# Retention attention and two MLP layers on one core: the last third of the first layer moved to a seven-product scheme, attention order, one slot pool

## The chip, the cores and the metric

One core of a Trainium2 chip runs the whole program in one launch. The metric is the device time of one execution in microseconds (us), lower is better. Engines: PE (TensorE, matmuls; PEld is its weight loads), DVE (VectorE), ACT (ScalarE), POOL (GpSimd), and SP, whose queue issues the DMAs. A line number such as L143 is a line of the kernel before; in the kernel after, the same statements stand some lines higher or lower.

## The reference

```python
# q, k, v: (4, 8, 576, 64)
gamma = 1.0 - 2.0 ** (-5.0 - np.arange(H))
Dmat = np.where(rel >= 0, gamma[:, None, None] ** rel, 0.0)   # rel = query - key position
x = ((q @ k^T) / 8 * Dmat) @ v                                # per batch and head, no softmax
x = x.transpose(0, 2, 1, 3).reshape(2304, 512)
h = x @ w_in ;  x = np.maximum(0.01 * h, h) @ w_out           # layer 1: 512 -> 2048 -> 512
h = x @ w2_in;  x = (h * sigmoid(h)) @ w2_out                 # layer 2, the same sizes
```

The weights arrive as float64 and are turned into float32 on the chip. All large matmuls are done at float32 precision by splitting each operand into a rounded part (hi) and a rest (lo) and adding three products, hi x hi, hi x lo, lo x hi (`PASSES`).

## The kernel before, in words

**Attention** works on eight units: for each of four batches the first 256 tokens (A) and the last 320 (B). A0 and A1 are done ahead of everything; the other six are cut into pieces (load, scale_k, products, outer, values) and put into the MLP's steps at the times in `ATT_AT` (L41). Its result goes into `X`, the 2304 tokens in the order of `UNITS` (L39), channels on partitions.

**Layer 1** runs over blocks of tokens, `BLOCKS` (L48): 512, 320, 512, 512, 448. A step is one block and one of the 16 slices f of the hidden layer: `gemm1` (L422, 12 matmuls into `h`), `activate` (L434: ACT leaky ReLU, ACT cast to hi, DVE rest lo into `g`), and `gemm2` two steps later (L444, 12 matmuls into `acc`). Each step also splits its two weight tiles, `wi` and `wo` (ACT cast, DVE subtraction; `split`, L119). In the first block the weights are also loaded and decoded (`decode`, L369). The first 32 steps stand in program order; from there to the end of the layer the scheduler chooses the order.

**Layer 2** takes 768 tokens at a time, three pairs of 384 (`PAIRS`, L30), in eight rounds k of two slices f each. The first product (X times w2_in) is done as a 2x2 block product with seven block products in place of eight: `sums_x` (L472) forms the sums of the X blocks and splits them, `sums_w` (L528) the same for the weights, `quad` (L576) issues the seven products of 6 matmuls x 384 columns into two PSUM banks `a` and `b`. Between products ACT copies bank `a` out (`snapshot`, L578), DVE adds bank `b` to such a copy (`add`, L584), and `finish` (L560) applies the activation and splits it into `gh` and `gl`. Snapshot, add and finish are marked high priority. A product that adds to bank `a` waits until the snapshot has read it. `outputs` (L614), 36 matmuls of 512 columns of the round before, fills the time between the products. PE and SP keep the program's order here; ACT and DVE are ordered by the scheduler. In the first pair the split weights are also written to DRAM (`kept`), and the later pairs fetch them from there. The weights of layer 2 are decoded in the last steps of layer 1 and in the first pair.

**Memory**: separate pools for raw weights, x splits, wi, wo, g, and after layer 1 new pools for the pairs (L847 to L851).

Of the kernel before, what the change touches and what calls it, by code (L numbers as in the profile page):

```python
# [22 lines left out]
LAG = 2  # L23
# [6 lines left out]
PAIRS = B * S // (2 * TILE)  # L30
# [17 lines left out]
BLOCKS = [[(0, 512), (512, 320), (832, 512), (1344, 512), (1856, 448)]]  # L48
# [15 lines left out]
def retention_mlp_kernel(ctx: ExitStack, tc: tile.TileContext, qkva, qkvb, w1, w2, consts, out):  # L64
# [4 lines left out]
    early = ctx.enter_context(ExitStack())  # L69
# [7 lines left out]
    wraw_p = pool("wraw", 1)  # L77
    x_p = pool("x", 1)
    xs_p = pool("xs", 6, stack=early)
    wi_p = pool("wi", 2, stack=early)  # L80
    wo_p = pool("wo", 2, stack=early)
    hs_p = pool("hs", 2, stack=early)
    g_p = pool("g", 3, stack=early)
    dec_p = pool("dec", 3, side=right)
    ld_p = pool("ld", 3, stack=heads, side=right)
# [6 lines left out]
    def slot(shape, dt, name, kind="wraw"):  # L92
        return wraw_p.tile(shape, dt, tag=kind, name=name, bufs={"wraw": NF - 7, "first": 7}[kind])
# [18 lines left out]
    gq2 = g_p.tile([128, NP, 2, CH], F32, tag="g", name="gq2")  # L112
# [73 lines left out]
    def products(u, ps):  # L186
# [29 lines left out]
        for i, p in enumerate(ps):  # L216
            k = [kv[p][:, c % 2, c // 2 * 64:(c // 2 + 1) * 64] for c in range(4)]
            if u[0] == "A":
                x = st_p.tile([128, 4, 64], F32, tag="st", name="st")
                sa = st_p.tile([128, 64], F32, tag="sa", name="sa", bufs=2 * NP)  # L220
# [58 lines left out]
    def end2(b, p, x):  # L279

        sa = st_p.tile([128, 64], F32, tag="sa", name="sa", bufs=2 * NP)
# [70 lines left out]
    def load_w(layer, f, parts=(0, 1)):  # L352

        if (layer, f) not in w64:
            wraw[layer, f] = slot([128, 1024], F32, "wraw", "first" if layer == 0 and f < 7 else "wraw")
# [44 lines left out]
    def split_wi(layer, i, f):  # L400

        w = wi_p.tile([128, 2, 512], F32R, tag="wi", name="wi")
# [3 lines left out]
    def split_wo(layer, i, f):  # L406

        w = wo_p.tile([128, 2, 512], F32R, tag="wo", name="wo")
# [3 lines left out]
    def split_x(layer, i, c, half=None, engine=nc.vector):  # L412
        p0, n = BLOCKS[layer][i]
        if not half:
            xs[layer, i, c] = xs_p.tile([128, 2, 512], F32R, tag="xs", name="xs")
# [6 lines left out]
    def gemm1(layer, i, f):  # L422
        n = BLOCKS[layer][i][1]
# [10 lines left out]
    def activate(layer, i, f):  # L434

        n = BLOCKS[layer][i][1]
        h = hidden.pop((layer, i, f))
        hs = hs_p.tile([128, 512], F32, tag="hs", name="hs")
        g = g_p.tile([128, 2, 512], F32R, tag="g", name="g")
# [4 lines left out]
    def gemm2(layer, i, f):  # L444
        p0, n = BLOCKS[layer][i]
# [26 lines left out]
    def sums_x(p):  # L472

        v = [[X[:, 2 * j:2 * j + 2, (2 * p + k) * TILE:(2 * p + k + 1) * TILE] for k in range(2)] for j in range(2)]
        b11, b12, b21, b22 = v[0][0], v[0][1], v[1][0], v[1][1]
        t1, t2, t4 = (xt_p.tile([128, 2, TILE], F32, tag="xt", name="xt") for _ in range(3))
        yield nc.vector.tensor_tensor(out=t1, in0=b12, in1=b11, op=ALU.subtract)
        yield nc.vector.tensor_tensor(out=b12, in0=b22, in1=b12, op=ALU.subtract)
        yield nc.vector.tensor_tensor(out=t2, in0=b22, in1=t1, op=ALU.subtract)
        yield nc.vector.tensor_tensor(out=t4, in0=b21, in1=t2, op=ALU.subtract)  # L480
        for name, x in (("b11", b11), ("b21", b21), ("t2", t2), ("t1", t1), ("t3", b12), ("t4", t4), ("b22", b22)):
            hi = xh_p.tile([128, 2, TILE], F32R, tag="xh", name="xh")
            yield nc.scalar.copy(out=hi, in_=x)
            lo = slot([128, 2, TILE], F32R, "xl", "first")
            yield nc.vector.tensor_tensor(out=lo, in0=x, in1=hi.bitcast(F32), op=ALU.subtract)
            xw[p, name] = hi, lo

    xw = {}
    ww = {}

# [4 lines left out]
    def weights(p, k):  # L495

        if (p, k) == (0, 0):
            homes = {"ha": (xt_p, "xt"), "la": (dec_p, "w64"), "hs": (xs_p, "xs"), "ls": (xs_p, "xs")}
        else:
            homes = {n: (wc_p, n) for n, _, _ in PARTS}  # L500
        t = {n: homes[n][0].tile([128, m, 256], F32R, tag=homes[n][1], name=n) for n, _, m in PARTS}
# [7 lines left out]
    def weights_out(p, k):  # L509

        wo = [wo2_p.tile([128, 2, 512], F32R, tag="wo", name="wo") for _ in range(2)]
        for i in range(2):
            wsp[1, p, 2 * k + i, 1] = wo[i]
            there = kept[k][:, 14 + 4 * i:18 + 4 * i]
            here = wo[i].bitcast(F32).rearrange("p a (b n) -> p (a b) n", b=2)
            if p:
                nc.sync.dma_start(out=here, in_=there)
            else:
                yield from split(wo[i][:, 0], wo[i][:, 1], wraw[1, 2 * k + i][:, 512:], nc.vector)
                nc.sync.dma_start(out=there, in_=here)  # L520
# [7 lines left out]
    def sums_w(p, k):  # L528
# [3 lines left out]
        w, z = wraw[1, 2 * k], wraw[1, 2 * k + 1]  # L532
        a = w[:, :512].rearrange("p (c n) -> p c n", c=2)
        yield nc.scalar.copy(out=ha[:, :2], in_=a)
        yield nc.vector.tensor_tensor(out=la[:, :2], in0=a, in1=ha[:, :2].bitcast(F32), op=ALU.subtract)
        s = [xt_p.tile([128, 2, 256], F32, tag="xt", name="ws") for _ in range(2)]
# [3 lines left out]
        yield nc.scalar.copy(out=hs[:, :2], in_=s[0])  # L540
# [406 lines left out]
```

## Time and profile before

| | us |
|---|---|
| median of 3 runs (lowest, highest) | 856.27 (856.17, 857.05) |
| the profiled execution: its own time | 856.27 |
| its span, first to last instruction | 854.4 |
| PE busy, of the span | 837.3 (98%) |
| DVE busy | 479.2 (56%) |
| ACT busy | 423.1 (50%) |
| POOL busy | 16.8 (2%) |

The profiled execution took 856.27 us, which is the median itself; 1.9 us of that lie outside the span. Busy shares are means over stages that differ: attention and decoding load DVE and ACT in the first 110 us and around the change from layer 1 to layer 2 (at about 464 us), and hardly in between or at the end.

### The profile page before, as it was taken

What the parts mean: (1) busy time and instruction counts of PE and PEld (TensorE: products, weight loads), DVE (VectorE), ACT (ScalarE), POOL (GpSimd) and SP (SyncE); (2) the same over time, 40 slices, a digit from 0 to 9 for tenths busy, and PEclk for the clock granted to TensorE, in tenths of its full rate; (3) what the DMA queues carried; (4) which work ended last, traced back from release to release, by engine and by line L of the source; (5) the groups of instructions that cost most, each with busy time, mean ns of one, the idle gap of its engine ahead of it and who ended that gap; (6) DMA issues with size and microseconds to landing.
All of it is one profiled execution on the core that took longest, in us unless ns stands there. A gap on an engine that the chain in (4) does not pass through costs nothing.

```text
span 854.4 us, 14185 instructions
## 1 busy us (share of the span) xinstructions
PE 837.3 (98%) x5784; PEld 724.2 (85%) x5784; DVE 479.2 (56%) x850; ACT 423.1 (50%) x762; POOL 16.8 (2%) x34
## 2 busy tenths in 40 slices
PE   8999999999999999999999899999999999999997
PEld 5678889998788878888999789999999999999995
DVE  6898856765455544545598689966322234322222
ACT  3788744454333443644475666655433435433332
POOL 5100000000000000000000000000000000000000
PEclk9999999999999999999999999999999999999999
DMA  9766533111111000000052599755564463754622
GB/s 338 277 223 242 175 114 107 59 66 58 50 58 66 2 33 2 1 0 1 1 185 99 209 398 363 285 195 212 213 234 169 170 234 140 272 207 138 227 92 74
DMA packets 38560, 127.94 MB, mean 150 GB/s; under 512 B 4320, under 2 KB 4448, under 8 KB 38496
## 3 DMA queue, kind: packets, MB, share of 16 engines
q1 hardware_dynamic: 38496, 127.05, 41.6%
q8 instruction: 45, 0.74, 0.3%
q14 instruction: 19, 0.16, 0.1%
HBM read 99.24 MB, written 27.79 MB: 149 GB/s over the span
## 4 chain that ended last, share of the span: by engine, by line
PE 87%; DVE 3%; DMA 2%; ACT 1%; SPq 0%; issue 0%; DVEq 0%; ACTq 0%
PE acc L143 36%; PE h L143 21%; PE a L143 11%; PE b L143 8%; PE att L143 7%; PE o L143 2%; PE r L143 2%; DMA qkv<-in_qkvb 1%; DMA w<-in_w 1%; SPq L359 0%; DVE wraw L397 0%; DVE w L381 0%; DVE gl L568 0%; ACT wo L121 0%; DVE wo L122 0%
## 5 line engine op out<-in xcount | busy, mean ns | idle before, releaser
L143 PE MATMUL h<-xs,wi 128*128 128x512 f32 (+2 forms) x960 | 218.6, 373 | 2.5 <-ACT wi L121 1.7
L143 PE MATMUL acc<-g,wo 128*128 128x512 f32 (+2 forms) x960 | 216.6, 371 | 0.2 <-DVE wo L122 0.2
L143 PEld LDWEIGHTS h<-xs,wi 128*128 128x128 f32 x960 | 171.0, 188 | 31.6 <-ACT wi L121 2.7
L143 PEld LDWEIGHTS acc<-g,wo 128*128 128x128 f32 x960 | 171.7, 188 | 26.8 <-DVE wo L122 0.6
L143 PE MATMUL acc<-wo,gh 128*128 128x512 f32 x384 | 134.0, 390 | 0.0
L586 DVE TENSOR_TENSOR X<-b,X 128x384 f32<-128x384 f32 x72 | 40.1, 558 | 141.0 <-ACT X L581 80.1
L441 ACT ACTIVATE hs<-h 128x512 f32<-128x512 f32 (+2 forms) x80 | 44.2, 553 | 111.2 <-PE h L143 108.7
L581 ACT COPY X<-a 128x384 f32<-128x384 f32 x72 | 34.6, 480 | 118.5 <-PE a L143 113.3
L121 ACT CAST wo<-wraw 128x512 fp32r<-128x512 f32 x96 | 59.3, 621 | 68.4 <-PE acc L143 66.2
L122 DVE TENSOR_TENSOR wi<-wraw,wi 128x512 fp32r<-128x512 f32 x78 | 53.7, 689 | 63.1 <-ACT wi L121 61.9
L122 DVE TENSOR_TENSOR wo<-wraw,wo 128x512 fp32r<-128x512 f32 x96 | 65.8, 688 | 38.4 <-ACT wo L121 38.3
L143 PEld LDWEIGHTS acc<-wo,gh 128*128 128x128 f32 x384 | 72.1, 188 | 12.9
L568 DVE TENSOR_TENSOR gl<-X,gh 128x384 fp32r<-128x384 f32 x96 | 53.4, 556 | 45.4 <-ACT gh L567 45.4
L143 PE MATMUL acc<-wo,gl 128*128 128x512 f32 x192 | 75.3, 392 | 0.8 <-DVE gl L568 0.8
L143 PE MATMUL att<-wo,gh 128*128 128x512 f32 x192 | 70.8, 390 | 0.0
L566 ACT ACTIVATE X<-X 128x384 f32<-128x384 f32 x72 | 37.8, 525 | 49.9 <-DVE X L586 49.7
L121 ACT CAST wi<-wraw 128x512 fp32r<-128x512 f32 x80 | 49.2, 615 | 13.4 <-DVE wraw L397 13.4
L122 DVE TENSOR_TENSOR g<-hs,g 128x512 fp32r<-128x512 f32 (+2 forms) x80 | 50.5, 631 | 9.2 <-ACT g L121 9.2
L567 ACT CAST gh<-X 128x384 fp32r<-128x384 f32 x96 | 49.1, 513 | 2.5
L121 ACT CAST g<-hs 128x512 fp32r<-128x512 f32 (+2 forms) x80 | 47.2, 590 | 0.7
L381 DVE TENSOR_SCALAR w<-w 128x512 uint16<-128x512 uint32 (+1 forms) x34 | 35.9, 1055 | 11.7 <-ACT wraw L376 11.7
L376 ACT ACTIVATE wraw<-w 128x1024 f32<-128x1024 f32 (+1 forms) x35 | 36.8, 1055 | 10.5 <-DMA w<-in_w 6.3
(115 smaller groups left out, 1103.9 us busy)
## 6 DMA issues: line engine op xcount, KB each, us to landing
w<-in_w SPq DMA_DIRECT2D x64, 512.0 KB, 5.6
wo<-kept SPq DMA_DIRECT2D x32, 512.0 KB, 7.0
qkv<-in_qkvb SPq DMA_DIRECT2D x16, 672.0 KB, 6.5
kept<-wo SPq DMA_DIRECT2D x16, 512.0 KB, 6.2
hs<-kept SPq DMA_DIRECT2D x16, 512.0 KB, 5.5
ls<-kept SPq DMA_DIRECT2D x16, 512.0 KB, 6.5
ha<-kept SPq DMA_DIRECT2D x16, 384.0 KB, 3.3
la<-kept SPq DMA_DIRECT2D x16, 384.0 KB, 3.9
```

The lines of the kernel that those rows point to most:

```text
L121: yield nc.scalar.copy(out=hi, in_=src)
L122: yield engine.tensor_tensor(out=lo, in0=src, in1=hi.bitcast(F32), op=ALU.subtract)
L143: return nc.tensor.matmul(out, lhsT, rhs, start=start, stop=stop, **kw)
L376: yield nc.scalar.mul(out=w, in_=hi.bitcast(F32), mul=2.0 ** -112)
L381: yield nc.vector.tensor_scalar(out=end[:, c], in0=lo[:, c].bitcast(U32), scalar1=2.0 ** -29, scalar2=7.0, op0=ALU.mult, op1=ALU.min)
L441: yield nc.scalar.activation(out=hs[:, :n], in_=h[:, :n], func=AF.Prelu, alpha=0.01)
L566: nc.scalar.activation(out=g, in_=h, func=AF.Silu)
L567: nc.scalar.copy(out=hi, in_=g)
L568: nc.vector.tensor_tensor(out=lo, in0=g, in1=hi.bitcast(F32), op=ALU.subtract)
L581: nc.scalar.copy(out=s, in_=a)
L586: nc.vector.tensor_tensor(out=s, in0=b, in1=s, op=ALU.add)
```

## The change

1. Layer 1 runs over three blocks of 512 tokens. Its last 768 tokens are done by the seven-product scheme as a pair of their own (p = 0), with leaky ReLU; layer 2's pairs become p = 1 to 3 (`PAIRS` is 4).
2. That pair's second product (`outputs_x`) keeps channels on partitions: per weight tile one matmul of 512 columns and one of 256, in place of matmuls of 320 and 448 columns in the blocks that are gone.
3. All A units come first, and the attention is done by step 43 of 48 (before: 57 of 80).
4. All 4 KB tiles come from one pool of 29 slots; x splits of the pairs from one of 14.
5. Layer 2's weights are decoded one a round in p = 0 and two a round in p = 1, half of one pass on ACT; `sums_x` of the next pair is spread over rounds 6, 7 and 0.
6. Snapshot, add and finish are no longer high priority. The last pair's odd output tiles are issued from ACT's queue. The ACT table with both activations is loaded once, at the start.

```diff
-PAIRS = B * S // (2 * TILE)
+PAIRS = 1 + B * S // (2 * TILE)
-UNITS = [("A", 0), ("A", 1), ("B", 0), ("B", 1), ("A", 2), ("B", 2), ("A", 3), ("B", 3)]
-ATT_AT = (2.8, 13.8, 13.8, 21, 21, 28, 28, 38, 38, 44, 45, 57)
+UNITS = [("A", 0), ("A", 1), ("A", 2), ("A", 3), ("B", 0), ("B", 1), ("B", 2), ("B", 3)]
+ATT_AT = (3.2, 8.4, 8.4, 13.8, 14, 22, 22, 29.8, 29.8, 36.5, 36.5, 43.1)
-BLOCKS = [[(0, 512), (512, 320), (832, 512), (1344, 512), (1856, 448)]]
+BLOCKS = [(0, 512), (512, 512), (1024, 512)]
...
-    xs_p = pool("xs", 6, stack=early)
-    wi_p = pool("wi", 2, stack=early)
+    s_p = pool("s", 29)
...
+    def first_of(p):
+        return NTOK - 2 * TILE if p == 0 else (p - 1) * 2 * TILE
...
     def finish(p, k, f, t, h):
-        with tc.high_priority():
+        if layer_of(p):
             nc.scalar.activation(out=g, in_=h, func=AF.Silu)
-            nc.scalar.copy(out=hi, in_=g)
-            nc.vector.tensor_tensor(out=lo, in0=g, in1=hi.bitcast(F32), op=ALU.subtract)
+        else:
+            nc.scalar.activation(out=g, in_=h, func=AF.Prelu, alpha=0.01)
+        run(split(hi, lo, g, nc.vector))
...
         def snapshot():
-            with tc.high_priority():
-                nc.scalar.copy(out=s, in_=a)
+            nc.scalar.copy(out=s, in_=a)
...
+    def outputs_x(p, f, g, w, end):
+        o = first_of(p)
+        units = [(m, wa, ga) for m in range(KC) for wa, ga in PASSES]
+        for n, (m, wa, ga) in enumerate(units):
+            ms = slice(m * 128, (m + 1) * 128)
+            last = end and (wa, ga) == PASSES[-1]
+            gather((p, m), acc[p][m // 2][:, m % 2], w[:, wa, ms], g[ga][:, :512], last)
+            gather((p, KC + m // 2), acc[p][2][:, m // 2, m % 2 * 256:m % 2 * 256 + 256], w[:, wa, ms], g[ga][:, 512:], last)
...
+                        (nc.scalar if p == PAIRS - 1 and e % 2 else nc.sync).dma_start(out=out[r:r + ln], in_=y[a:a + ln])
...
-            if t == t0 + NF - 4:
-                run(x0)
-                w0 = sums_w(0, 0)
+            if t == len(steps) - 4:
+                attend(t + 1)
+                heads.close()
+                x2_p = pool("x2", 14, side=right, stack=second)
+                x0 = sums_x(0)
+                w0 = sums_w(0, 0)
...
-    for st in steps[-LAG:]:
-        for _ in gemm2(*st):
-            pass
+    left = itertools.chain(*(gemm2(*st) for st in steps[-LAG:]))
+    decoded = {0: (0, 1, 1, 1, 1, 1, 1, 0), 1: (0, 2, 2, 2, 2, 2, 0, 0)}
...
+                if j in (0, 2) and todo:
+                    todo -= 1
+                    run(decode(*wdec.pop(0), 512))
+                    more_weights(nw + 1)
```

What the scheduler makes of it, at three places. **PE, the end of layer 1.** Before, the last block's steps (`h` is gemm1's bank, `acc` gemm2's):

```order
L143 MATMUL acc_4178<-g,wo 128x448 x6
L143 MATMUL acc_4179<-g,wo 128x448 x6
L143 MATMUL h<-xs,wi 128x448 x12
L143 MATMUL acc_4178<-g,wo 128x448 x2
L143 MATMUL acc_4179<-g,wo 128x448
```

Now, in a round of p = 0 (`att` is the third bank pair, `gh` and `gl` the split activation):

```order
L138 MATMUL acc_3661<-gh,wo 128x512
L138 MATMUL att<-gh,wo 128x256
L138 MATMUL acc_3661<-gl,wo 128x512
L138 MATMUL att<-gl,wo 128x256
L138 MATMUL acc_3661<-gh,wo 128x512
L138 MATMUL att<-gh,wo 128x256
```

The 384 matmuls of 448 columns and the 384 of 320 are gone; 336 of 384 columns, 192 of 512 and 192 of 256 have come. No other matmul's count changed.

**PE, the entry into the first pair.** Before, from the last gemm1 on (`xh`, `ha`: the hi parts of `sums_x` and `sums_w`):

```order
L143 MATMUL h<-xs,wi 128x448 x10
L143 MATMUL acc_4178<-g,wo 128x448 x6
L143 MATMUL acc_4179<-g,wo 128x448 x6
L143 MATMUL a<-xh,ha 128x384
L143 MATMUL acc_4178<-g,wo 128x448 x2
L143 MATMUL acc_4179<-g,wo 128x448 x2
L143 MATMUL a<-xl,ha 128x384
```

Now, from the end of the attention's last piece (`o<-qkv,st`) on:

```order
L138 MATMUL o<-qkv,st 64x64 x16
L138 MATMUL h<-xs,wi 128x512 x8
L138 MATMUL acc_2689<-g,wo 128x512 x6
L138 MATMUL acc_2690<-g,wo 128x512 x6
L138 MATMUL acc_2689<-g,wo 128x512 x6
L138 MATMUL acc_2690<-g,wo 128x512 x4
L138 MATMUL h<-xs,wi 128x512 x2
L138 MATMUL acc_2690<-g,wo 128x512 x2
L138 MATMUL a<-xh,ha 128x384
```

The first product now stands before the last gemm1 is finished, and the X that it needs comes from the attention instead of an evacuated layer 1.

**ACT, a round with decoding** (`wraw<-w` and `w<-w,seven` are decode's two ACT passes, `COPY X<-a` the snapshots). Before, in round 3 of the first pair, from the second snapshot to the third:

```order
L581 COPY X<-a 128x384
L566 ACTIVATE X<-X 128x384
L544 CAST hs<-ws 128x512
L567 CAST gh<-X 128x384
L376 ACTIVATE wraw<-w_5225 128x1024
L581 COPY X<-a 128x384
```

Now, in round 3 of p = 0; rounds 4 to 6 of p = 0 and 1, 3 and 5 of p = 1 read alike:

```order
L590 COPY X<-a 128x384
L116 CAST wo<-wraw 128x512
L116 CAST hs<-ws 128x512 x2
L371 ACTIVATE wraw<-w_3701 128x1024
L382 ACTIVATE w_3701<-w_3701,seven 128x512
L590 COPY X<-a 128x384
```

Between the two snapshots ACT now has three casts of 512 and both decode passes; before it had one such cast, an activation with its cast, and one decode pass.

## Rows read from the trace of the kernel before

**Rows 1.** The page: busy time, and a group of weight loads.

```profile
PE 837.3 (98%) x5784; PEld 724.2 (85%) x5784; DVE 479.2 (56%) x850; ACT 423.1 (50%) x762; POOL 16.8 (2%) x34
...
L143 PEld LDWEIGHTS h<-xs,wi 128*128 128x128 f32 x960 | 171.0, 188 | 31.6 <-ACT wi L121 2.7
```

**Rows 2.** Windows: start:end, us, each engine's busy time (instructions), clock, DMA share, GB/s.

```profile
35.85:106.45 70.60, 69.02 (x584) 54.31 (x585) 62.80 (x118) 56.92 (x82) 1.16 (x2) 1.00 0.66 232
463.69:512.44 48.75, 44.99 (x223) 39.73 (x222) 37.56 (x64) 31.79 (x62) 0.00 (x0) 1.00 0.70 265
527.90:543.50 15.60, 15.60 (x80) 14.14 (x79) 14.44 (x25) 9.93 (x19) 0.00 (x0) 1.00 0.93 325
```

**Rows 3.** Chain of waits, four stretches: start us, us, what, how many in a row.

```profile
133.79 1.76 PE acc L143 x12
...
358.23 2.72 PE h L143 x12
...
407.92 2.43 PE acc L143 x12
...
606.13 1.05 PE a L143 x6
```

**Rows 4.** Groups by form, PE: matmuls that go, and the attention's.

```profile
L143 PE MATMUL h<-xs,wi 128*128 128x448 f32 x192 | 41.7, 365 | 0.0
...
L143 PE MATMUL h<-xs,wi 128*128 128x320 f32 x192 | 33.0, 314 | 0.3 <-DVE xs L122 0.3
...
L143 PE MATMUL r<-qkv 64*64 64x64 f32 x896 | 17.6, 222 | 0.1
...
L143 PE MATMUL o<-pt,qkv 64*64 64x64 f32 x448 | 13.7, 230 | 0.0
L143 PE MATMUL o<-qkv,st 64*64 64x64 f32 x352 | 7.7, 218 | 0.0
```

**Rows 5.** Chain of waits, 463 to 503 us, entry into layer 2.

```profile
471.68 2.07 ACT wo L121 x4
473.75 0.39 ACT X L581
```

**Rows 6.** Timeline of ACT, a step with decoding: start us, us, instruction.

```profile
66.87 1.13 ACT L376 ACTIVATE wraw<-w 128x1024 f32<-128x1024 f32 x1
67.89 0.59 ACT L441 ACTIVATE hs<-h 128x512 f32<-128x512 f32 x1
68.37 1.48 ACT L387 ACTIVATE w<-w,seven 128x512 uint16<-128x512 uint32 x1
69.58 0.69 ACT L121 CAST g<-hs 128x512 fp32r<-128x512 f32 x1
```

**Rows 7.** Groups by form, DVE: the attention's pieces.

```profile
L287 DVE SCALAR_TENSOR_TENSOR st<-st,cst,r 128x64 f32<-128x64 f32 x64 | 18.0, 281 | 2.2
...
L212 DVE TENSOR_TENSOR pt<-r,mask 128x384 f32<-128x384 f32 x16 | 8.8, 553 | 0.7 <-PE r L143 0.7
...
L184 DVE TENSOR_TENSOR qkv<-qkv,cst 128x256 f32<-128x256 f32 x20 | 8.4, 422 | 19.1 <-DMA qkv<-in_qkvb 11.1 <-DMA qkv<-in_qkva 7.9
...
L330 DVE TENSOR_TENSOR X<-o,cst 128x640 f32<-128x640 f32 x8 | 6.6, 820 | 5.6 <-PE o L143 5.6
...
L212 DVE TENSOR_TENSOR pt<-r,mask 128x256 f32<-128x256 f32 x8 | 3.0, 416 | 0.0
...
L330 DVE TENSOR_TENSOR X<-o,cst 128x512 f32<-128x512 f32 x4 | 2.8, 690 | 3.3 <-PE o L143 3.3
```

**Rows 8.** Timeline of PE at step 16, the first of the second block.

```profile
119.28 1.65 PE L143 MATMUL h<-xs,wi 128*128 128x320 f32 x10
121.26 0.56 PE L143 MATMUL h<-xs,wi 128*128 128x320 f32 x2 [0.34 <-DVE xs L122]
```

**Rows 9.** Timeline of the end: the last output tiles.

```profile
847.95 1.73 SPq L636 DMA_DIRECT2D out<-y  x3
...
850.40 0.40 SPq L636 DMA_DIRECT2D out<-y  x1
```

More of the change, by code (lines that the diff above doesn't have):

```diff
@@ L354, in load_w @@
         if (layer, f) not in w64:
-            wraw[layer, f] = slot([128, 1024], F32, "wraw", "first" if layer == 0 and f < 7 else "wraw")
+            wraw[layer, f] = slot([128, 1024], F32, "wraw")
             w64[layer, f] = dec_p.tile([128, 1024, 2], I32, tag="w64", name="w64")
@@ L400, in split_wi @@
     def split_wi(layer, i, f):
-        w = wi_p.tile([128, 2, 512], F32R, tag="wi", name="wi")
+        w = slot([128, 2, 512], F32R, "wi")
         wsp[layer, i, f, 0] = w
@@ L495, in weights @@
     def weights(p, k):
[L497 to L501, printed above, removed]
+        t = {n: slot([128, m, 256], F32R, n) for n, _, m in PARTS}
         ha, la, hs, ls = t.values()
@@ L509, in weights_out @@
     def weights_out(p, k):
[L511 removed]
         for i in range(2):
[L513 removed]
+            f = 2 * k + i
+            wsp[p, f] = w = slot([128, 2, 512], F32R, "wo")
             there = kept[k][:, 14 + 4 * i:18 + 4 * i]
[L515 to L516 removed]
+            here = w.bitcast(F32).rearrange("p a (b n) -> p (a b) n", b=2)
+            if p > 1:
                 nc.sync.dma_start(out=here, in_=there)
             else:
[L519 to L520 removed]
+                yield from split(w[:, 0], w[:, 1], wraw[p, f][:, 512:], nc.vector)
+                if p:
+                    nc.sync.dma_start(out=there, in_=here)
     def fetch(p, k):
@@ L531, in sums_w @@
         ha, la, hs, ls = t.values()
-        w, z = wraw[1, 2 * k], wraw[1, 2 * k + 1]
+        w, z = wraw[p, 2 * k], wraw[p, 2 * k + 1]
         a = w[:, :512].rearrange("p (c n) -> p c n", c=2)
-        yield nc.scalar.copy(out=ha[:, :2], in_=a)
-        yield nc.vector.tensor_tensor(out=la[:, :2], in0=a, in1=ha[:, :2].bitcast(F32), op=ALU.subtract)
-        s = [xt_p.tile([128, 2, 256], F32, tag="xt", name="ws") for _ in range(2)]
+        yield from split(ha[:, :2], la[:, :2], a, nc.vector)
+        s = [hs_p.tile([128, 2, 256], F32, tag="hs", name="ws") for _ in range(2)]
         s1, s2, s3, s4 = (s[i // 2][:, i % 2] for i in range(4))
@@ L612, in retention_mlp_kernel, with gather @@
     started = set()
+    def gather(bank, o, w, x, last):
+        mm(o, w, x, bank not in started, last, skip_group_check=True)
+        started.add(bank)
     def outputs(p, k):
         if k == 0:
-            t = [q.tile([128, 2, 512], F32, tag=n, name=n) for q, n in ((acc_p, "acc0"), (acc_p, "acc1"), (att_p, "att"))]
-            acc[1, p] = [t[m // 2][:, m % 2] for m in range(6)]
+            acc[p] = [q.tile([128, 2, 512], F32, tag=n, name=n) for q, n in ((acc_p, "acc0"), (acc_p, "acc1"), (att_p, "att"))]
+        end = k == NF // 2 - 1
@@ L639, in retention_mlp_kernel @@
-    places = itertools.cycle([None, X[:, 2, :512], None, X[:, 3, :512], None])
-    def place():
-        y = next(places)
-        return y_p.tile([128, 512], F32, tag="y", name="y") if y is None else y
+            g, w = gp[p, k, f], wsp[p, 2 * k + f]
+            yield from (outputs_x if layer_of(p) == 0 else outputs_y)(p, f, g, w, end and f == 1)
+    def outputs_x(p, f, g, w, end):
+        o = first_of(p)
+        units = [(m, wa, ga) for m in range(KC) for wa, ga in PASSES]
[4 more added lines that the diff above has]
+            gather((p, KC + m // 2), acc[p][2][:, m // 2, m % 2 * 256:m % 2 * 256 + 256], w[:, wa, ms], g[ga][:, 512:], last)
+            if last and m % 2:
+                for e in (m - 1, m):
+                    evacuate(X[:, e, o:o + 512], acc[p][m // 2][:, e % 2], e % 2)
+            if last and m == KC - 1:
+                for e in range(2):
+                    evacuate(X[:, 2 * e:2 * e + 2, o + 512:o + 768], acc[p][2][:, e].rearrange("p (e n) -> p e n", e=2), e)
+            if n % 2:
+                yield
@@ new lines, in outputs_y @@
+    def outputs_y(p, f, g, w, end):
+        for n in range(6):
+            o = acc[p][n // 2][:, n % 2]
+            for wa, ga in PASSES:
+                gather((p, n), o, g[ga][:, n * 128:(n + 1) * 128], w[:, wa], end and (wa, ga) == PASSES[-1])
+            if end and n % 2:
+                for e in (n - 1, n):
+                    y = slot([128, 512], F32, "y")
+                    evacuate(y, acc[p][e // 2][:, e % 2], e % 2)
+                    for a, ln, r in rows_of(first_of(p) + e * 128, 128):
+                        (nc.scalar if p == PAIRS - 1 and e % 2 else nc.sync).dma_start(out=out[r:r + ln], in_=y[a:a + ln])
+            yield
```

196 lines of the change are left out of this document (87 added, 109 removed).

## The prediction, made before the kernel was run

> **What bounds the kernel now.** I read the page's busy table first: PE is busy for 837.3 of 854.4 us, DVE for about half of the span [rows 1]. So the time is PE's work plus the few stretches in which PE stands, and the clock is 1.00 in every window that I use [rows 2]. Next, the chain of waits: almost the whole of it is PE rows, and runs of equal matmuls in it give PE's pace, start to start. 12 of 512 columns take 2.72 us (226.7 ns each), 12 of 448 take 2.43 us (202.5), 12 of 320 take 1.76 us (146.7), 6 of 384 take 1.05 us (175) [rows 3]. The durations of the groups (365 ns for 448 columns, 314 for 320 [rows 4]) overlap from one matmul to the next and are no price; all sums below go by pace. Third, the windows, to find the stretches with gaps. The entry into layer 2 lasts 48.75 us [rows 2]; two of the stretches that PE waits in are behind ACT's queue and behind a late decode. The early attention, steps 3 to 13, lasts 70.60 us, with DVE busy for 62.80 of it [rows 2]. A clean round of a pair lasts 15.60 us with PE never waiting [rows 2].
>
> 0.2% of the time is 1.7 us, about what a measurement of this kernel can tell from no change. The profiled execution took 856.27 us, the median of the three runs, so the sum needs no shift; the 1.9 us outside the span are taken as kept.
>
> **The change part by part.**
>
> *The last 768 tokens of layer 1.* Removed are 384 matmuls of 448 columns and 384 of 320: 384 x 0.2025 + 384 x 0.1467 = 77.8 + 56.3 = 134.1 us [rows 3]. Added are eight rounds of p = 0, each 42 matmuls of 384, 24 of 512 and 24 of 256. The clean round of now has the same 42 and 36 of 512, so a new one is 15.60 - 12 x 0.2267 + 24 x t, where t is the pace of 256 columns. No row has it. From 512 to 320 columns the pace falls by 80.0 ns for 192 columns, so 26.7 ns for 64: 120.0 ns at 256, which I take (from 448 to 320 alone it would be 118.8). Then a round is 15.60 - 2.72 + 2.88 = 15.76 us, eight are 126.1, and the term is **-8.0 us**. From below t is bounded by 256 columns at the full 2.4 GHz, 107 ns: 2.6 us less. From above by the nearest row, 320 columns at 147 ns: 5.1 us more.
> By the Trainium skill ("TensorE: Matmul & The Clock Gate", Back-to-back issue gap) an isolated gap is the columns at 2.4 GHz plus 2.5 ns, 109 ns here, and the term would be -10.1 us; the paces of this trace lie 13 to 16 ns above columns at 2.4 GHz [rows 3], so the measurement decides.
>
> *The entry into the first pair.* Between 463.69 and 512.44 us PE issues work worth 42 x 0.175 + 24 x 0.2025 = 12.2 us and two rounds, 31.2: 43.4 of 48.75, so 5.3 us are lost [rows 2, 3]. One piece is seen in the chain: a snapshot starts only at 473.75, behind four casts of `wo` that hold ACT for 2.07 us, and the next product waits for it [rows 5]. In the changed order those weights are split a round ahead, decoding is one tile a round, and the first product's X comes from the attention's last piece: the 34 matmuls of 512 columns between that piece and the product last 7.7 us, and the X needs one multiplication of 640 columns (0.82 us [rows 7]) and three steps of 768 columns, each some 1.0 us by the 0.82 scaled up: 3.8 us. It is ready in time. I take all of the loss as gone: **-5.3 us**; the bound is 0, if it comes back at the new entry.
>
> *The queue of ACT.* Snapshots are no longer ahead of other work. In seven rounds (3 to 6 of p = 0; 1, 3, 5 of p = 1) ACT has between the second and third snapshot three casts and both passes of decode: by the paces of a decoding step, 3 x 0.5 (start to start of `hs`, 0.48) + 1.02 + 1.21 = 3.7 us, by their durations some 4.5 [rows 6]. Between the product whose bank the second snapshot reads and the one that waits for the third, PE issues two products and 15 matmuls of outputs: 2.1 + 3.4 = 5.5 us [rows 3]. Two snapshots of 0.39 [rows 5] and the 3.7 make 4.5 us: it fits if the second snapshot is on time, and by durations, with the second snapshot 0.9 us late behind its own neighbours, PE waits 0.8. Round 0 of p = 1, where `sums_x` still runs, is short by some 0.7 us by the same sum. I take 0.7 and 0.1 for each of the seven: **+1.4 us**; bounds 0 and 0.7 + 7 x 0.8 = 6.3.
>
> *The early attention.* In steps 3 to 13 two A units (A2, A3) take the place of one B unit. By DVE's rows [rows 7]: per unit, the 16 state operations are alike; A has 4 masks at 0.416 and 2 results at 0.69, B 4 at 0.553 and 2 at 0.82; A3's four scalings at 0.422 stay on DVE, those of A2 and B0 run on ACT. With a state operation at 0.28, A2 is 7.5, A3 9.2, B0 8.4: DVE gets 8.4 us more. PE gets more as well: the attention's matmuls are 39.0 us [rows 4] for 1792 tokens, and 192 tokens more make 4.2 us, taken from later steps. So PE's window is 74.8 us and DVE's work 71.2: it fits barely. DVE's idle 7.8 us were partly forced (it waited for PE or ACT); were all of it, the window would be 71.2 + 7.8 = 79.0, 4.2 over. I take a quarter: **+1.0 us**, since the pieces can slide into the next steps; bounds 0 and 4.2.
>
> *Block edges.* At step 16 PE now has a block of 512 columns. Before, it waited 0.34 us there with 320 [rows 8]. The split of four chunks grows by about what PE's cover grows; two of the four edges vanish, one gets wider: **+0.3 us**, bounds -0.5 and +0.5.
>
> *The end.* SP issues the last tiles one behind the other, three in 1.73 us from 847.95, the last at 850.40 [rows 9]. With every second one on ACT's queue one slot of 0.58 goes: **-0.6 us**, bounds 0 and -0.9.
>
> *At nothing:* the other attention pieces (all matmuls kept, moved under gemms, DVE idle half of the later span [rows 1]); the table load at the start (in the shadow of the first transfers); the kept writes and reads of weights, one pair later each: a round with DMA at 325 GB/s ran without a wait of PE [rows 2], and without that cover each late tile would hold its product; the one pool of 29 slots, whose waits are for tiles read a round ago, and whose failing would show as DMA waits on PE.
>
> Sum: -8.0 - 5.3 + 1.4 + 1.0 + 0.3 - 0.6 = -11.2, so **845.0 us**.
>
> **The rivals.**
>
> 1. *A matmul of 256 columns is no cheaper than one of 320.* It changes the weights as often, and each load is recorded with 188 ns [rows 1]. For it: no row is narrower than 320 with a full weight tile. Against: 320 runs at 147, below 188, so loads overlap. 192 x 0.0267 = +5.1: 850.1 us.
> 2. *The change doesn't do what it says at the entry:* the 5.3 us stay, since p = 0 needs decode, split and sums in its first rounds as pair 0 did. For: the same work in the same place of a pair. Against: the order of the queues. 850.3 us.
> 3. *ACT's queue replaces the stall:* snapshots wait in order behind casts and decode in all seven rounds, as at 471.68 [rows 5]. Against: the sum above fits. 845.0 - 1.4 + 6.3 = 849.9 us.
> 4. *DVE bounds the early steps:* 4.2 in place of 1.0: 848.2 us.
> 5. *Slower:* the weight load becomes the bound. In `outputs_x` each load serves one matmul of 256 columns in turn; if a load can't overlap more than the one matmul ahead, a 256 takes 188 + 2 = 190 ns: 192 x 0.070 = +13.4, 858.4 us. It decides from t = 188 ns on, where the gain is all but gone. Against: loads of 188 ns under matmuls at 147.
> By the Trainium skill ("TensorE: Matmul & The Clock Gate", LDWEIGHTS) a load takes its columns at 1.2 GHz, 107 ns for 128, so it would hide under 256 columns and this rival would fall; the trace here has only the 188 ns of its records.
>
> **How the numbers follow.** Chances: forecast 0.57 (its own range 841 to 848), rivals 0.12, 0.08, 0.12, 0.08 and 0.03. Rivals 1 to 4 alone are all faster by over 1.7 us; two or three of them together (0.05 of their 0.40) end near 855 or above, within 0.2%. So faster 0.92, same 0.05, slower 0.03. The low end of the range is the forecast with t = 107 ns and a queue that costs nothing: 845.0 - 2.6 - 1.4 = 841.0. The high end, 851.0, takes in each single rival up to 850.3; left out are rival 5, the combinations, and some 0.07 below.
>
> **What would show it.** In the changed profile: the pace of the outputs in a clean round of p = 0, a 512 and a 256 in turn, 347 ns for the two; a round there of 15.8 us; a PE window from the last gemm1 of layer 1 to the second round with a loss below 1 us; ACT waits of PE's product `a` behind snapshots below 0.2 us a round, largest at round 0 of p = 1; DVE near 95% in steps 3 to 13 with PE waiting on `h` or `acc` for under 1.5 us there; SP's last issue within 2 us of the last copy. A pace of 147 or 190 ns for 256 columns makes rival 1 or 5 true; a product that waits over 3 us for a late split or transfer in rounds 0 and 1 of p = 0, rival 2.

## The result, and the profile of the changed kernel

| | before | changed |
|---|---|---|
| median, us (lowest, highest; runs) | 856.22 (855.98, 857.05; 4) | 847.81 (846.30, 848.40; 4) |
| profiled execution, us (span) | 856.27 (854.4) | 846.30 (844.6) |
| PE busy, us | 837.3 | 828.4 |

The ratio of changed to before is 0.9897, 95% interval 0.988 to 0.9915: 7 to 10 us faster. Forecast were 845.0 in a range of 841 to 851, and faster. The profiled execution is the fastest of the four, 1.5 us under their median; the spread matters below.

The page's busy line of the changed kernel, against [rows 1]:

```profile
PE 828.4 (98%) x5736; PEld 713.2 (84%) x5736; DVE 486.3 (58%) x908; ACT 445.0 (53%) x783; POOL 17.7 (2%) x34
```

PE is busy 8.9 us less in a span that is 9.8 us shorter. Windows of the changed kernel (start:end, length, busy time and instructions of PE, PEld, DVE, ACT, POOL, granted clock, DMA share, GB/s): steps 0 to 13, the first two rounds of p = 0, and a later round of p = 0.

```profile
22.89:113.49 90.60, 85.89 (x797) 66.64 (x793) 80.11 (x161) 66.08 (x96) 3.61 (x7) 0.98 0.60 210
328.74:361.61 32.87, 31.77 (x167) 28.28 (x166) 26.23 (x51) 22.99 (x43) 0.00 (x0) 1.00 0.01 2
377.40:393.19 15.79, 15.79 (x93) 14.72 (x92) 11.03 (x22) 10.62 (x19) 0.00 (x0) 1.00 0.27 91
```

A round of p = 0 lasts 15.79 us with PE never idle (15.76 forecast). In the chain of waits of such a round the outputs run so (start, us, what):

```profile
376.18 0.23 PE acc L138
376.40 0.12 PE att L138
376.52 0.23 PE acc L138
```

256 columns take 0.12 us, as extrapolated. So the main term holds. Two stretches stayed worse than forecast. First, the entry into p = 0 (PE's and ACT's timeline; in brackets the idle time ahead of a row and what ended it):

```profile
332.27 0.60 ACT L436 ACTIVATE hs<-h 128x512 f32<-128x512 f32 x1 [1.06 <-PE h L138]
...
332.92 0.44 PE L138 MATMUL b<-xh,ha 128*128 128x384 f32 x1 [0.69 <-ACT hs L436]
...
347.02 0.51 ACT L116 CAST gh<-X 128x384 fp32r<-128x384 f32 x1
...
347.59 0.50 PE L138 MATMUL acc<-gh,wo 128*128 128x512 f32 x1 [0.41 <-ACT gh L116]
```

Product `b` takes the bank of the last `h`, which ACT has only begun to read; and the first outputs wait for a `gh` that the end of round 0 made late, because no matmul of layer 1 was left to stand between the last products. Start to start these two cost 0.85 and 0.57 us. By the sum that gave the forecast its 5.3 us (the window, less 42 of 384 columns at 0.175, 34 left ones of 512 at 0.2267 and a round of 15.79), 2.0 us are lost, since the first matmuls behind each wait take 0.1 us more each: 32.87 - 30.85.

Second, the early attention. DVE and PE around the first outer piece of A2:

```profile
49.55 0.69 DVE L117 TENSOR_TENSOR wi<-wraw,wi 128x512 fp32r<-128x512 f32 x1
...
50.16 0.75 DVE L207 TENSOR_TENSOR pt<-r,mask 128x256 f32<-128x256 f32 x2
...
52.79 0.28 DVE L282 SCALAR_TENSOR_TENSOR sa<-st,cst,r 128x64 f32<-128x64 f32 x1
...
53.22 0.46 PE L138 MATMUL o<-pt,qkv 64*64 64x64 f32 x16 [1.34 <-DVE sa L282]
```

The outer piece writes the bank that the products filled (there is one, `att`), so it waits until DVE has read all of it: for an A unit two masks, two copies and six state operations, 2.9 us from 50.16 to 53.07, in order behind the step's decoding and its `wi`. And PE ran slowly just before (windows):

```profile
43.00:44.00 1.00, 0.99 (x3) 0.48 (x3) 1.00 (x4) 1.00 (x4) 0.00 (x0) 1.00 0.96 344
44.00:46.00 2.00, 2.00 (x66) 1.72 (x66) 2.00 (x9) 2.00 (x5) 0.00 (x0) 0.63 0.86 272
46.00:48.00 2.00, 2.00 (x5) 1.61 (x6) 1.51 (x4) 1.97 (x3) 0.00 (x0) 0.51 0.66 246
48.00:50.00 2.00, 2.00 (x10) 1.60 (x10) 1.85 (x3) 1.11 (x3) 0.00 (x0) 1.00 0.14 20
```

The granted clock was at its lower level, 1.2 GHz, for about 3.4 us, from 1.5 us behind the end of a wait of 1.65 us; matmuls of 512 columns came 427 ns apart. In the profile of the kernel before, which has a wait of 1.57 us in the same place, the clock is 1.00 in all these windows. By the Trainium skill ("TensorE: Matmul & The Clock Gate", Back-to-back issue gap) the spacing at the lower clock is the columns at 1.2 GHz, 426.7 ns for 512: the trace agrees.

### The profile page after: what moved, and what is told of

Its sections match the earlier page's. It is cut to its first block, busy times and chain, and to the rows that moved or that the text cites. A ratio compares the mean times of both kernels' runs of the same rounds, so it can differ in the third digit from the quotient of the medians.

```text
span 844.6 us, 14065 instructions
## 1 busy us (share of the span) xinstructions
PE 828.4 (98%) x5736; PEld 713.2 (84%) x5736; DVE 486.3 (58%) x908; ACT 445.0 (53%) x783; POOL 17.7 (2%) x34
## 4 chain that ended last, share of the span: by engine, by line
PE 90%; DVE 1%; ACT 0%; issue 0%
PE acc L138 35%; PE a L138 16%; PE h L138 13%; PE b L138 12%; PE att L138 10%; PE o L138 2%; PE r L138 2%; DVE st L282 0%; DVE pt L207 0%; DVE wraw L392 0%; DVE y L460 0%; DVE xs L117 0%; ACT hs L436 0%; DVE g L117 0%; DVE wi L117 0%
## 5 line engine op out<-in xcount | busy, mean ns | idle before, releaser
L138 PE MATMUL h<-xs,wi 128*128 128x512 f32 x576 | 147.2, 400 | 2.9 <-ACT wi L116 1.7
L138 PE MATMUL acc<-g,wo 128*128 128x512 f32 x576 | 142.5, 393 | 0.0
L138 PEld LDWEIGHTS h<-xs,wi 128*128 128x128 f32 x576 | 106.0, 189 | 28.9 <-ACT wi L116 2.5
L138 PEld LDWEIGHTS acc<-g,wo 128*128 128x128 f32 x576 | 106.9, 188 | 22.6
L117 DVE TENSOR_TENSOR g<-hs,g 128x512 fp32r<-128x512 f32 x48 | 33.1, 690 | 66.1 <-ACT g L116 66.1
L138 PE MATMUL acc<-gh,wo 128*128 128x512 f32 x128 | 48.6, 396 | 0.4 <-ACT gh L116 0.4
L382 ACT ACTIVATE w<-w,seven 128x512 uint16<-128x512 uint32 x30 | 44.0, 1466 | 0.4
L138 PE MATMUL a<-xh,hs 128*128 128x384 f32 x128 | 43.4, 339 | 0.0
L138 PE MATMUL b<-xh,hs 128*128 128x384 f32 x128 | 43.4, 339 | 0.0
L138 PE MATMUL a<-xh,ha 128*128 128x384 f32 x128 | 43.4, 339 | 0.0
```

Source lines behind the costliest of these rows:

```text
L117: yield engine.tensor_tensor(out=lo, in0=src, in1=hi.bitcast(F32), op=ALU.subtract)
L138: return nc.tensor.matmul(out, lhsT, rhs, start=start, stop=stop, **kw)
L382: yield nc.scalar.activation(out=end[:, c], in_=lo[:, c].bitcast(U32), func=AF.Relu, scale=-2.0 ** -29, bias=seven)
```

## The experiments

Each has its own profile, and its runs were taken beside runs of the kernel before on the same chip, whose medians lie between 856.3 and 856.6 us; so times of different experiments compare to within some 0.5 us. Times are medians, intervals 95%.

**1. The changed kernel once more**

> The changed kernel once more, unchanged, for a second profile. Its four runs went from 846.3 to 848.4 us, and the profiled one was the lowest. Theory (the spread is in the first 75 us, where the granted clock fell to 0.51 for some 4 us after a wait of 1.65 us): in this profile the rounds from p = 0 to the end are as long as in the other within 0.1 us each, and the difference of the two spans lies before 110 us. Rival (the spread comes from transfers or waits in the later rounds): a round of p = 1 to 3 differs by over 0.3 us. Median expected 847 to 848.5.

847.83 us (846.90 to 848.20). Its profile has a span of 846.4, 1.8 us more. Before the outer piece PE waits longer, and the clock falls after it (PE's timeline, then a window):

```profile
52.88 0.70 PE L138 MATMUL o<-pt,qkv 64*64 64x64 f32 x16 [2.88 <-DVE sa L282]
53.51 5.49 PE L138 MATMUL h<-xs,wi 128*128 128x512 f32 x12
```

```profile
50.00:75.00 25.00, 22.12 (x208) 17.48 (x208) 20.84 (x47) 17.64 (x26) 1.02 (x2) 0.86 0.62 208
```

The 12 matmuls of `h` take 5.49 us, where at the full clock they would take 2.9. Steps 0 to 13 last 91.93 us here, 1.3 more than in the first profile; 0.5 us of the rest are at the ends of rounds 3 and 5 of p = 1, which last 15.77 and 15.91 us (15.59 in the first profile). So most of the difference lies before 110 us, as the theory said, but not all, and the rival has a part.

**2. One part alone: the kernel before with the A units first**

```diff
-UNITS = [("A", 0), ("A", 1), ("B", 0), ("B", 1), ("A", 2), ("B", 2), ("A", 3), ("B", 3)]
+UNITS = [("A", 0), ("A", 1), ("A", 2), ("A", 3), ("B", 0), ("B", 1), ("B", 2), ("B", 3)]
-ATT_AT = (2.8, 13.8, 13.8, 21, 21, 28, 28, 38, 38, 44, 45, 57)
+ATT_AT = (3.2, 8.4, 8.4, 13.8, 14, 22, 22, 29.8, 29.8, 36.5, 36.5, 43.1)
```

> The kernel before (856.2 us) with one part of the change alone: the A units first, with the changed kernel's times of the attention, one more load buffer and all states kept. Theory (the attention's new order costs the early steps about 3.5 us): 859.0 to 860.5 us, with PE waiting over 1 us before two outer pieces in steps 4 to 8. Rival (the early loss of the changed kernel's profile is a chance of the clock and of transfers, and not of the order): 856 to 857 us. Forecast of the prediction (+1.0): 857.2.

858.34 us, ratio 1.0025 (1.0015 to 1.0034): 2 us slower, less than the theory's 859.0 and more than the rival's 857.0. The wait came (PE's timeline):

```profile
53.47 0.56 PE L143 MATMUL o<-pt,qkv 64*64 64x64 f32 x16 [2.85 <-DVE sa L287]
53.96 1.65 PE L143 MATMUL h<-xs,wi 128*128 128x512 f32 x3
```

So the order of the attention alone costs it, and 3 matmuls in 1.65 us show the low clock again. Part of the loss came back at the end, which experiment 6 explains.

**3. A units cut like B units**

```diff
-        if u[0] == "A":
-            return [(scale_k, (u, p)) for p in ps] + [(products, (u, ps)), (outer, (u, g)), (values, (u, g))]
```

> The changed kernel (847.8 us), but the A units are cut as the B units are: the products of the two head pairs of a group are two pieces instead of one, so that between the last product and the outer piece DVE has one mask and four state operations instead of two masks and eight. Theory (the early loss is the length of DVE's chain between products and outer, which stand less than a step apart): the two waits of PE before an outer piece, 1.5 us at 51.5 and 1.2 us at 70.1 in the changed kernel's profile, fall below 0.5 each; the time falls by 1 to 2.5 us, to 845.3 to 846.8. Rival (DVE is short of throughput in steps 3 to 13, whatever the order): the waits move to other matmuls, time within 0.7 us of the changed kernel. Second rival (each piece more costs PE a switch between the small and the large matmuls): 0.5 us more for each of four pieces, so 1 to 2 us slower.

850.83 us, 3.0 slower than the changed kernel. The waits before outer pieces went, as the theory had it, but three others came: one of 2.5 us before a products piece at 50.56 (the profile names no cause; DVE's last reading of the bank ends at 50.45), and two inside a products piece, for ACT's scaling of k (PE's timeline):

```profile
43.86 0.74 PE L138 MATMUL r<-qkv 64*64 64x64 f32 x16 [2.33 <-ACT qkv L175]
...
70.67 0.74 PE L138 MATMUL r<-qkv 64*64 64x64 f32 x16 [2.06 <-ACT qkv L175]
```

These two pieces take 3.46 and 3.20 us start to start, others of the same 32 matmuls 0.62: 5.4 us more. The switches of the second rival are the smaller part: two pieces of 32, with the way to and from the large matmuls, take 1.64 us where one of 64 takes 1.29, four times, 1.4 us. So the waits moved to other matmuls, as the first rival said, though its 0.7 us were not kept; the experiment tells little of DVE's throughput.

**4. The outer piece later**

```diff
-                queue.append((at, (f, x)))
+                queue.append((at + (0.45 if f == outer and u[0] == "A" else 0), (f, x)))
```

> The changed kernel (847.8 us), but the outer pieces of the A units that are spread over steps 3 to 13 stand 0.45 of a step later, behind a whole gemm1 of 12 matmuls (2.7 us). In the second profile of the changed kernel PE waits 3.0 us before the first outer piece, at 49.6, and from 53.5 on its clock is at 1.2 GHz for 11 matmuls, 0.2 us each more. Theory (DVE's chain between products and outer comes too late for the place of the outer piece; the wait brings the clock down): the wait falls below 0.6, the clock stays at 1.00 from 43 to 75 us, 3 to 5 us faster: 843 to 845. Rival (DVE is short of throughput): the wait moves on to the next matmuls that need DVE, within 1 us of 847.8. Second rival (the clock falls anyway, by the earlier waits of 0.8 and 1.3 us): 2 to 2.5 us faster with the clock below 0.9 somewhere from 41 to 60 us: 845.3 to 845.8.

845.23 us, 2.6 less than the changed kernel, between the bands of the theory and of its second rival. What is left of the wait, and the clock:

```profile
52.87 0.46 PE L138 MATMUL o<-pt,qkv 64*64 64x64 f32 x16 [0.18 <-DVE sa L282]
...
54.62 1.65 PE L138 MATMUL acc<-g,wo 128*128 128x512 f32 x6 [0.62 <-DVE wo L117]
```

```profile
50.00:62.00 12.00, 11.20 (x98) 8.31 (x97) 10.77 (x24) 8.23 (x12) 0.26 (x1) 1.00 0.52 167
```

DVE's work is the same; only the place of the outer piece moved, by 12 matmuls. The wait falls from some 3.0 to 0.34 us start to start, 0.8 us come back before `acc`, and the clock stays up. Steps 0 to 13 last 88.30 us, in place of 90.60 and 91.93. These are 5.1 more than the 83.19 of the kernel before, of which 3.6 are the attention's added work (see the account of that term below), so 1.5 are left. So DVE nearly had the throughput; what it lacked was distance between products and outer.

**5. Priority for snapshot, add and finish again**

```diff
+            with tc.high_priority():
-            nc.scalar.copy(out=s, in_=a)
+                nc.scalar.copy(out=s, in_=a)
```

(the same around `add` and in `finish`)

> The changed kernel (847.8 us) with snapshot, add and finish marked as high priority again. Theory (ACT's queue costs PE nothing in the 15 rounds that last 15.59 or 15.79 us, and only the 0.6 us at the first outputs of p = 0, where an add of DVE stands behind another tile's work): 0 to 0.6 us faster, 847.2 to 847.8. Rival (the term of the prediction, +1.4 us for the queue of ACT, stands): 1.4 us faster, 846.4. Second rival (with priority the casts and decodes are late instead): slower by 0.5 us or more.

847.50 us, 0.3 less than the changed kernel and inside the spread. But the edit changed nothing that ran: in this profile and in the changed kernel's PE (5736 instructions), ACT (783), DVE (908) and POOL (34) run the same instructions in the same order, from first to last. So this is one more execution of the changed kernel and decides between none of the three. That the waits at the entry stay at 0.85 and 0.57 us says nothing of ACT's or DVE's order.

ACT's queue is not free, though. In the profiles of experiments 1, 6, 7 and 8 rounds 3 and 5 of p = 1 lose 0.4 to 1.4 us together. ACT and PE in round 3 of experiment 6 (SP alone), from the end of round 2 on:

```profile
501.54 1.13 ACT L371 ACTIVATE wraw<-w 128x1024 f32<-128x1024 f32 x1 [1.24 <-DMA w<-in_w]
...
508.43 0.53 ACT L574 ACTIVATE X<-X 128x384 f32<-128x384 f32 x1 [2.36 <-DVE X L594]
...
511.64 1.15 ACT L116 CAST hs<-ws 128x512 fp32r<-128x512 f32 x2
...
512.69 1.14 ACT L371 ACTIVATE wraw<-w 128x1024 f32<-128x1024 f32 x1
...
513.86 1.46 ACT L382 ACTIVATE w<-w,seven 128x512 uint16<-128x512 uint32 x1
...
515.06 0.58 ACT L590 COPY X<-a 128x384 f32<-128x384 f32 x1
...
515.69 0.44 PE L138 MATMUL a<-xh,ha 128*128 128x384 f32 x1 [0.49 <-ACT X L590]
```

That is rival 3's mechanism, in two of its seven rounds and in some executions only: the product whose bank it copies ended at 513.1, its snapshot began at 515.06, behind decoding, and PE waited 0.65 us start to start. What makes ACT late is the first line: the decode at the end of round 2 waits 1.24 us for the transfer of its raw weight, and ACT and DVE, whose orders are the same in the changed kernel's first profile, come late from there on, by way of DVE's add. In that first profile the same decode starts without a wait:

```profile
499.23 1.15 ACT L371 ACTIVATE wraw<-w 128x1024 f32<-128x1024 f32 x1
```

The eleven profiles with the changed kernel's rounds have 22 such places (before rounds 3 and 5 of p = 1). In the 12 where the decode waits 0 to 0.42 us for its transfer, PE loses nothing in the next round; in the other 10, with waits of 0.52 to 1.24, it loses that wait less 0.43 to 0.47 us. Why the transfers land differently stays open.

**6. Output tiles from SP alone; the kernel before once more**

```diff
-(nc.scalar if p == PAIRS - 1 and e % 2 else nc.sync).dma_start
+nc.sync.dma_start
```

> The changed kernel (847.8 us), but with all output tiles issued from SP again, as before the change. The stretch from the last matmul's start to the span's end was 6.73 us before and is 6.00 now. Theory: 6.6 to 6.8 again, 0.6 to 0.8 us slower, 848.4 to 848.6. Rival (the shorter end has another reason, the evacuation by ACT and DVE): 6.0, no change.

> The kernel before, unchanged, for a second profile. From the last matmul's start to the end of the span its profile shows 6.73 us; the changed kernel's profiles show 5.96 to 6.07 with two queues, 5.81 with SP alone, and the kernel before with another attention order 5.85. Theory (the end differs from execution to execution, and the prediction's term for it was read from one): 5.8 to 6.8, not 6.73 again, median 856 to 857. Rival (the end of the kernel before is 6.7 in each execution): 6.7. The entry loses 5.0 to 5.5 us again, and the clock is 1.00 in all windows to 75 us if the early waits stay below 1.7 us each.

With SP alone 847.61 us, no slower. The end, from the last matmul's start, is 5.81 us, against 6.01 with two queues and 6.73 before; the kernel before once more (856.82 us) shows 6.75, so it does not vary by chance: both theories fell. (Its clock is 1.00 to 75 us, as expected, with no early wait over 1.1 us; the 1.7 us in that expectation is no limit that a run shows, since the changed kernel's clock fell after 1.65. Its entry lost 6.9 us by the prediction's sum, more than expected, for a reason given further below.) The kernel before with A first has 5.85 with SP alone. The difference is in SP's list of transfers at the end. The kernel before has eight (first fence), that with A first seven (second), as has the changed kernel with SP alone:

```profile
847.13 0.34 SPq L636 DMA_DIRECT2D out<-y  x1
847.85 1.11 SPq L636 DMA_DIRECT2D out<-X  x2
849.06 1.74 SPq L636 DMA_DIRECT2D out<-y  x3
850.89 0.55 SPq L636 DMA_DIRECT2D out<-X  x1
851.53 0.39 SPq L636 DMA_DIRECT2D out<-y  x1
```

```profile
849.90 0.34 SPq L636 DMA_DIRECT2D out<-y  x1
850.63 0.34 SPq L636 DMA_DIRECT2D out<-X  x1
851.26 1.84 SPq L636 DMA_DIRECT2D out<-y  x3
853.19 0.54 SPq L636 DMA_DIRECT2D out<-X  x1
853.82 0.40 SPq L636 DMA_DIRECT2D out<-y  x1
```

A tile of 128 tokens that lies across two units is written in two pieces. In the last pair the old order of units splits two of the six tiles, the new one one (a unit now ends at token 1664, a multiple of 128). So the 0.9 us come from the order of the units, and the second queue costs 0.2 of them again; that the count of transfers is the reason is what the lists suggest, no run changed it alone.

**7. Three matmuls of 256 in a row**

```diff
-            gather((p, m), acc[p][m // 2][:, m % 2], w[:, wa, ms], g[ga][:, :512], last)
+            for i in range(2):
+                gather((p, m), acc[p][m // 2][:, m % 2, i * 256:i * 256 + 256], w[:, wa, ms], g[ga][:, i * 256:i * 256 + 256], last)
```

> The changed kernel (847.8 us), but each matmul of 512 columns of the second product of p = 0 is cut into two of 256, so that three of 256 stand in a row for each weight tile and 192 matmuls are added. Now a 512 and a 256 take 350 ns. Theory (a matmul of 256 columns takes its columns at 2.4 GHz and some 13 ns; its weight load lies under the matmul before): three take 351 to 360 ns, so 0 to 2 us slower, 847.8 to 849.8. Rival (the load of 188 ns hides only because a matmul of 512 stands beside it; in a row of 256 each takes about 190): 570 ns for three, 192 x 0.22 = 42 us slower, 890. Between them: if matmuls with the same weights need no second load, 256 after 256 shows two paces.

848.71 us, 0.9 more. A clean round of p = 0:

```profile
378.92:394.91 15.99, 15.99 (x116) 15.99 (x115) 10.99 (x22) 10.66 (x19) 0.00 (x0) 1.00 0.25 84
```

Less 42 x 0.175 that is 8.64 us for 72 matmuls of 256: 120.0 ns each, with a weight load of their own before each. Rivals 1 (147) and 5 (190) are out, beside a 512 as beside another 256. The Trainium skill ("TensorE: Matmul & The Clock Gate", LDWEIGHTS) gives 107 ns for such a load; that loads hide in a row of 120 ns agrees, and the 188 ns of the records [rows 1] are no interval.

**8. Another spread of the left matmuls at the entry**

```diff
         c11 = snapshot()
+        y0, y1, y2, y3 = (1, 2, 1, 2) if (p, k) == (0, 0) else (0, 3, 2, 3)
+        if y0:
+            yield y0
         product(b, p, k, "a12", "b21", True)
...
-        yield 3
+        yield y1
...
-        yield 2
+        yield y2
...
-        yield 3
+        yield y3
```

> The changed kernel (847.8 us), but the matmuls that are left of layer 1's second product are spread over round 0 of p = 0 in another way: three stand ahead of the second block product, whose bank is read by ACT until 332.9 (a wait of 0.85 us now), and six between the last two products, behind which the first outputs wait 0.57 us for gh. Theory (what is left of the entry's loss is a bank and a latency that PE's order leaves uncovered): both waits go, 1.0 to 1.4 us faster, 846.4 to 846.8. Rival (the late DVE and ACT work at the entry sets the end, and the waits move to another product): within 0.4 us of 847.8.

846.33 us, 1.5 less, a little beyond the theory's band. Both waits are gone: the first two rounds last 15.42 and 15.75 us, in place of 16.10 and 16.77, 1.7 less. PE's order made them.

**9. Together**

The two edits of 4 and 8; with the snapshots' priority besides; and with the split of the last two chunks of X at a block's edge in one step:

```diff
-                run(split_x(l2, i2, f - (NF - KC)))
+                c = f - (NF - KC)
+                for c in (c,) if c < 2 else (2, 3) if c == 2 else ():
+                    run(split_x(l2, i2, c))
```

> The changed kernel (847.8 us) with the outer pieces 0.45 of a step later and the other spread of the left matmuls at the entry, both at once; alone they gave 845.2 and 846.3. Theory (they stand in different stretches, 49 to 75 and 329 to 349 us, and add): 843.7, range 843.0 to 844.5. Rival (what one saves the other gives back, since DVE's late work sets the entry): 844.8 or more.

> The same two and the snapshots alone marked as high priority. In four of six profiles with p = 1 in the changed order PE waited 0.2 to 1.1 us in all at the ends of rounds 3 and 5 of p = 1, for the third snapshot, which stands behind wo, two hs and both decode passes. Theory (rival 3 of the prediction holds for these two rounds, in some executions): no such wait, 0.3 to 0.6 us faster than without, 843.1 to 843.4. Rival (decode is then late and a later product waits): no gain or slower.

> As the one before, and the split of the last chunk of X at a block's edge is issued a step earlier, with the third. In all profiles of the changed order PE waits 0.69 us at step 16 for DVE's split of that chunk. Theory (the split stands last in DVE's order and only its place makes PE wait): the wait goes, 0.5 to 0.7 us faster, 842.5 to 842.9. Rival (DVE is busy to the edge, the wait comes back before another matmul): no change.

843.63, 843.36 and 842.66 us. The first and the last step fell in their bands: the savings of 4 and 8 add, and the wait at step 16, which the changed kernel's first profile shows so, is gone (step 16 lasts 6.16 us, 7.0 in the others).

```profile
129.27 0.74 PE L138 MATMUL h<-xs,wi 128*128 128x512 f32 x2 [0.53 <-DVE xs L117]
```

The priority again changed no engine's order, so the first two kernels are the same in what runs, and their 0.3 us are spread; the second one's profile lost 0.5 us in rounds 3 and 5 of p = 1, behind decodes that waited 0.82 and 0.52 us for their transfers. The last kernel's ratio is 0.9838 (0.9824 to 0.9852): 13.7 us faster than before and 5 faster than the change.

## Why the prediction came out as it did

| term | forecast, us | measured, us |
|---|---|---|
| last 768 tokens by seven products | -8.0 | -7.8: eight rounds of 15.79 against 134.1 |
| entry stalls | -5.3 | -3.3: 2.0 left by the same sum, 1.4 of it in two waits |
| ACT's queue | +1.4 | 0 in the first profile, 0.4 to 1.4 in experiments 1, 6, 7 and 8 |
| early attention on DVE | +1.0 | +3.8 and +5.2 in two profiles |
| block edges | +0.3 | +0.2: 0.8 at step 16 against 0.6, none at the others |
| other attention pieces | at nothing | -1.6: two pieces that the scheduler had broken up |
| the end | -0.6 | -0.7, by another cause |

Measured terms add up to -9.4 in the first profile, whose span is 9.8 shorter (steps begin 0.4 earlier, an amount that differs from execution to execution). In the second they are -7.8 - 3.3 + 0.5 + 5.2 + 0.2 - 1.6 - 0.7 = -7.5, with a span 8.1 shorter. The median lies between. So the median fell into the range, but in part because terms that were missed have opposite signs: the early attention cost 2.8 to 4.2 us more than forecast and the entry gave 2.0 less, against 1.6 that came unforeseen. These 1.6 are two values pieces of the kernel before, at 196 and 306 us, each of which its scheduler had cut in three around large matmuls; a whole piece takes 1.28 us with its switches, these took 2.0 and 2.1.

*The seven products* were sized rightly, to 0.03 us a round. Experiment 7 shows why extrapolation was safe: with a load before each matmul, nothing in the load of weights binds down to 256 columns.

*The entry* was taken as wholly gone. The step that failed is "It is ready in time": the sum asked when X is ready, and X was. It did not ask for the bank of the second product, nor what stands between the last products of round 0 when all left matmuls are spent. Both stand in the order of PE ahead of the run; experiment 8 shows that they set the wait. The loss in the kernel before differs too: its second profile needs 50.32 us where the first needs 48.75 [rows 2], since the clock fell there in the middle of the waits (window):

```profile
476.00:478.00 2.00, 2.00 (x8) 2.00 (x8) 0.57 (x2) 1.15 (x3) 0.00 (x0) 0.50 0.04 12
```

*The early attention* is the term that was mis-sized, and rival 4 came true, with another mechanism: "I take a quarter ... since the pieces can slide into the next steps". They cannot: the pieces' places in PE's order are fixed, and an outer piece holds all gemms behind it. The bound of 4.2 us came from DVE's busy time, and the first profile's size is within it by coincidence (the second's is not); experiment 4 shows that a move by 0.45 step, with DVE's load unchanged, removes most, and experiment 2 that the order of the units alone brings it (90.56 us for steps 0 to 13, 90.60 in the changed kernel). The clock is part of the price and was in no term: after a wait of 3.0 us some 6 to 11 matmuls of 512 columns cost 0.2 us more each, 1.5 to 2.7 us in all. PE's added work was over-sized as well: the prediction took the attention's 39.0 us of busy time, which by its own word is no price. Start to start, with the switches, the eight pieces of one B unit take 7.7 us and the twelve of two A units 11.3, so 3.6 are added and not 4.2. For the measured numbers I took the 83.19 us of steps 0 to 13 in the kernel before and these 3.6, 86.8, from 90.60 and 91.93. Experiment 4's 88.30 is then +1.5, near the forecast.

*ACT's queue* was right in where PE would wait and wrong in why. Its sum of 5.5 us against 4.5 said that the snapshots fit if the second one is on time, and otherwise cost some 0.8 us. That is what happened, in two of the seven rounds and in some executions: in round 3 of experiment 6 the second snapshot is 1.0 us later in its round than in the first profile, and PE loses 0.8. But what delays it is a raw weight that lands late, and the cover of transfers stood at nothing, with failing expected as waits of PE; here they are waits of ACT. That the missing priority matters is not shown: experiment 5 put the marks back and the order stayed.

*The end*: "With every second one on ACT's queue one slot of 0.58 goes" failed. The size was near by chance; the cause is the order of the units, which leaves one transfer less, and with it the second queue gained nothing (5.81 us without it, 6.01 with it).

*Rival 2* came true in size by over a third (2.0 of 5.3), but not by its mechanism: the waits come from PE's order and not from late decoding, split or sums. *1 and 5* are out, *3* came in part, *4* in size but not in mechanism. The median is 2.8 us above the forecast.

## What to carry to other kernels

When a piece of work moves, look in the fixed order of the waiting engine for what stands between its producer and its consumer, and for the bank that it reuses: busy shares tell whether the work fits, only the distance tells whether it waits. A wait inside a dense stream of matmuls can cost more than itself, since the clock may fall after it. Follow a late engine back to the first thing that it waited for: ACT's late snapshots began with a transfer, some 14 us earlier. Before an experiment is read, compare the order in which the engines ran: an edit that leaves it as it was tests nothing. And name a term's cause so that one run can refute it: the end's size was right and its cause wrong.

## What the runs showed of the hardware

After a wait of PE of 3.0 to 3.1 us (experiments 1, 2, 5, 6 with SP alone, 7 and 8) the granted clock went to 1.2 GHz in six profiles of six, 0.7 us before the wait's end (experiments 1 and 7) or within 1.7 us behind it, and came back after 6 to 11 matmuls of 512 columns. After waits of 1.0 to 1.65 us near 41 us it fell in two profiles (1.65 in the first of the changed kernel, 1.63 in the first of experiment 9) and not in eleven others, one of them with 1.64; after three of 2.2 to 2.5 us (experiment 3) it did not fall. At the entry of the kernel before it fell after two waits of 1.4 and 0.7 us in the second profile and not after the same two in the first. So the length of the wait alone does not decide, and what else does stays open. It is also a part of the spread between executions: the profiles of one kernel differ in whether and where the clock fell.

A decode on ACT that waited over 0.43 us for its raw weight cost PE the rest of that wait some 14 us later, through two engines that run in a fixed order (experiment 5).

Of two output queues at the end, one was enough: seven transfers of 256 KB or less issued from SP take 4.32 us, and the end is 0.2 us shorter than with four of them on ACT's queue.
